# Attention scores from split q and k: a stacked two-pass product against three products on each head's own 64 rows

## The chip, the cores and the metric

The kernel runs on one core of one Trainium2 chip. The metric is device time in microseconds of one execution. TensorE (PE) multiplies matrices into PSUM, VectorE (DVE), ScalarE (ACT) and GpSimd (POOL) work on tiles, and SyncE (SP) issues nearly all DMA transfers, in order.

## What is computed

Softcapped attention over 4 batches, 12 heads, 448 positions and a head dimension of 64, then a bilinear feed-forward layer over all 1792 tokens:

```python
scores = scale * np.matmul(q, k.transpose(0, 1, 3, 2))
scores = cap * np.tanh(scores / cap)
attn = np.exp(scores - np.max(scores, axis=-1, keepdims=True))
attn = attn / (np.sum(attn, axis=-1, keepdims=True) + 1e-09)
x = np.matmul(attn, v)            # laid out as (1792, 768)
out = (x @ w_a) * (x @ w_b) @ w_out
```

q, k, v are f32. The weights arrive as 64-bit floats, and the kernel makes f32 out of them itself.

## The kernel before

**Precision.** A fp32r matmul passes once over its moving columns, at less than f32 precision. Where f32 precision is wanted, an operand x is split into a high part hi (x rounded to fp32r) and a low part lo = x - hi, and three one-pass products hi·hi, hi·lo and lo·hi are added up in PSUM. Matmuls on plain f32 tiles take several passes; the trace counts two instructions for each.

**Units of work.** The 48 heads are taken in 24 pairs, two heads A and B on partitions 0 to 63 and 64 to 127. Twelve pairs make a token group of 896 rows (`NG` = 2). The feed-forward of group 0 (`ffn(0)`) runs in slices between the steps of pairs 12 to 23, and that of group 1 (`ffn(1)`) runs behind the last pair. So there are three stages: attention alone (pairs 0 to 11), attention mixed with feed-forward and with the conversion of the weights, and feed-forward alone.

**Steps of one pair.** `load_pair` fetches q, k, v. `prep_pair` transposes q and k so that the head dimension lies on partitions, and splits them. `scores(pi, 0)` makes key chunks 0 and 1 (128 keys each) for both heads, `scores(pi, 1)` chunk 2 and the remainder of 64 keys. Each chunk goes into a PSUM tile `psc` of two banks, one per head (the remainder's two heads share one bank, one on each half of the partitions), and ACT takes tanh (L270) and then exp (L271). POOL and DVE add up the row sums in `psum`. `attend` (L293, L295) multiplies by v into `pv`, and `normalize` adds the sums over partitions (L308), takes the reciprocal (L316), spreads it through DRAM (`rd`, `den`), multiplies (L322) and splits the result into `xhi`, `xlo` (L331, L332) for the feed-forward.

**Transposes.** For pairs up to 12 (`pi < BLOCKED`) q and k are loaded with 112 partitions and transposed on PE against an identity (L232). From pair 13 on they are loaded in 32-wide column blocks (L206, eight issues), and one VectorE instruction per tensor transposes all 32x32 blocks (L223).

**Scores before.** `keys` holds for head A its high parts on rows 0 to 63 and its low parts on rows 64 to 127, for head B the other way round; `qhh` holds the high part of q on both halves. So one matmul over 128 rows (L263) gives hi·hi + lo·hi, and a second over the own 64 rows (L264) adds hi·lo. The other half of `qhh` is filled by a copy on DVE (L240, first two pairs) or by an SBUF-to-SBUF DMA (L242). The remainder's 64 keys of both heads take two matmuls over windows that reach into columns of zeros between the heads (L268), and a third with `kdiag`, the remainder's high parts on a diagonal (L269).

**Order.** The program's order for a pair is given by a string of steps, `"PASNFTF"` up to pair 12 and `"SFANPFTF"` after (P prep of the next pair, A and N attend and normalize of the pair before, S and T the two score halves, F a slice of feed-forward). The framework's scheduler puts each engine's instructions in order from there; on each engine they run in that order. `psc` tiles come from a pool of two (`ps_sc`), which from pair 12 on also holds `pv`; other PSUM tiles come from a pool of four (`ps_1`). Split q and k, `psum` and the probabilities are double-buffered.

**Weights.** In the first pass each of 36 weight tiles is converted (L389 to L394: two ACT, three DVE, one POOL instruction), written to DRAM, and split (L411, L412); in the second pass it is read back.

Of the kernel before, what the change touches and what calls it, by code (L numbers as in the profile page):

```python
# [9 lines left out]
F32 = mybir.dt.float32  # L10
# [106 lines left out]
def kernel(  # L117
# [66 lines left out]
    # [0 | B's first R] put both heads' remainders in one bank; kdiag has their high parts on its diagonal.  # L184
    koff, krem = (0, S + R), (MAIN, S + R)
    keys = [const.tile([P, 2 * S + R], F32R, tag=f"keys{i}", name=f"keys{i}") for i in range(2)]
    kdiag = [const.tile([P, P], F32R, tag=f"kdiag{i}", name=f"kdiag{i}") for i in range(2)]
    xhi = const.tile([P, NK, GT], F32R, tag="xhi", name="xhi")
    xlo = const.tile([P, NK, GT], F32R, tag="xlo", name="xlo")
    acc = const.tile([P, NTI, DM], F32, tag="acc", name="acc")  # L190

    un = lambda ap: ap.rearrange("d (p c) -> d c p", c=NCH)
    pm = lambda ap: ap.rearrange("d (c p) -> d c p", c=NCH)
    sides = ((slice(0, D), slice(D, P)), (slice(D, P), slice(0, D)))
    raw, stk, prob, pvs = {}, {}, {}, {}

    def load_pair(pi):
        b, hp = divmod(pi, NP)
        for nm, src in (("k", k), ("q", q)):
            if pi >= BLOCKED:  # L200
                t = ld.tile([P, S // BLK, BLK], F32, tag=f"ld{nm}", name=f"ld{nm}_{pi}")
                for j in range(2):
                    for h in range(D // BLK):
                        rows = slice(j * D + h * BLK, j * D + (h + 1) * BLK)
                        cols = src[b, 2 * hp + j, :, h * BLK : (h + 1) * BLK]
                        nc.sync.dma_start(t[rows], cols.rearrange("(c p) d -> p c d", p=BLK))  # L206
                raw[nm, pi] = t
                continue
            t = ld.tile([CP, NCH, 2, D], F32, tag=f"ld{nm}", name=f"ld{nm}_{pi}")
            for j in range(2):  # L210
                nc.sync.dma_start(t[:, :, j, :], src[b, 2 * hp + j].rearrange("(p c) d -> p c d", c=NCH))
            raw[nm, pi] = t
        t = ld.tile([P, 2 * NC3 + 1, D], F32, tag="ldv", name=f"ldv_{pi}", bufs=3)
        nc.sync.dma_start(t, v[b, 2 * hp : 2 * hp + 2].rearrange("j s d -> (j s) d").rearrange("(c p) d -> p c d", p=P))
        raw["v", pi] = t

    def prep_pair(pi):
        tk, tq = raw.pop(("k", pi)), raw.pop(("q", pi))
        blocked = pi >= BLOCKED
        if blocked:  # L220
            pk, pq = (qk.tile([P, S], F32, tag=f"t{nm}", name=f"t{nm}_{pi}", bufs=1) for nm in "kq")
            for p_, t in ((pk, tk), (pq, tq)):
                nc.vector.transpose(p_, t.rearrange("p c d -> p (c d)"))  # L223
        else:
            if pi >= NPG:
                both = ps_sc.tile([P, 2, 512], F32, tag="pssc", name=f"pt_{pi}")
                pk, pq = both[:, 0], both[:, 1]
            else:
                pk, pq = (ps_1.tile([P, 512], F32, tag="ps1", name=f"pt{nm}_{pi}") for nm in "kq")
            for p_, t in ((pk, tk), (pq, tq)):  # L230
                for c in range(NCH):
                    nc.tensor.transpose(p_[:, c * CP : (c + 1) * CP], t[:, c].rearrange("p j d -> p (j d)"), ident[:CP, :CP])  # L232
        khl, kdg = keys[pi % 2], kdiag[pi % 2]
        qhh = qk.tile([P, 2, S], F32R, tag="qhh", name=f"qhh_{pi}")
        qlo = qk.tile([P, S], F32R, tag="qlo", name=f"qlo_{pi}")
        to, fr = (lambda x: x, lambda x: x) if blocked else (un, pm)
        for j, (own, oth) in enumerate(sides):
            nc.scalar.copy(to(qhh[own, j]), fr(pq[own, :S]))
            if pi < 2:
                nc.vector.tensor_copy(un(qhh[oth, j]), pm(pq[own, :S]))  # L240
            else:
                nc.sync.dma_start(f32(qhh[oth, j]), f32(qhh[own, j]))  # L242
        for j, (own, oth) in enumerate(sides):
            kj = khl[:, koff[j] : koff[j] + S]
            nc.vector.tensor_copy(to(kj[own]), fr(pk[own, :S]))
            eng = nc.gpsimd if blocked else nc.vector
            eng.tensor_sub(to(kj[oth]), fr(pk[own, :S]), to(f32(kj[own])))
            nc.gpsimd.tensor_copy(kdg[own, j * R : (j + 1) * R], f32(khl[own, krem[j] : krem[j] + R]))
        for j, (own, oth) in enumerate(sides):
            nc.vector.tensor_sub(to(qlo[own]), fr(pq[own, :S]), to(f32(qhh[own, j])))  # L250
        stk[pi] = (khl, kdg, qhh, qlo)

    def scores(pi, hf):
        khl, kdg, qhh, qlo = stk[pi]
        pf = pp.tile([P, 4 - hf, S], F32, tag=f"pf{hf}", name=f"pf_{pi}_{hf}")
        for i in range(2):
            c = 2 * hf + i
            n = 2 if c < NC3 else 1
            psc = ps_sc.tile([P, 2, 512], F32, tag="pssc", name=f"psc_{pi}_{c}")
            if n == 2:  # L260
                for j, (own, _) in enumerate(sides):
                    kc = khl[:, koff[j] + j * R + c * P : koff[j] + j * R + (c + 1) * P]
                    nc.tensor.matmul(psc[:, j, :S], kc, qhh[:, j], start=True, stop=False)  # L263
                    nc.tensor.matmul(psc[:, j, :S], kc[own], qlo[own], start=False, stop=True)  # L264
            else:
                for j in range(2):
                    kc = khl[:, MAIN + j * R : MAIN + j * R + P]
                    nc.tensor.matmul(psc[:, 0, :S], kc, qhh[:, j], start=(j == 0), stop=False)  # L268
                nc.tensor.matmul(psc[:, 0, :S], kdg, qlo, start=False, stop=True)  # L269
            nc.scalar.activation(pf[:, 2 * i : 2 * i + n], psc[:, :n, :S], AF.Tanh, scale=capt[:, 1:2])  # L270
        nc.scalar.activation(pf, pf, AF.Exp, scale=capt[:, 0:1])  # L271
        prob[pi, hf] = pf
        t = psum[pi % 2]
        if hf == 0:
            nc.gpsimd.tensor_add(t, pf[:, 0:2], pf[:, 2:4])
        else:
            for j, (own, _) in enumerate(sides):
                nc.vector.scalar_tensor_tensor(  # L278
                    t[own, j], pf[own, 2], capt[own, 2:3], t[own, j], op0=ALU.add, op1=ALU.add
                )  # L280
            nc.gpsimd.tensor_add(t, t, pf[:, 0:2])  # L281

    def attend(pi):
        if pi >= NPG:
            both = ps_sc.tile([P, 2, 512], F32, tag="pssc", name=f"pv_{pi}")
            pvs[pi] = (both[:, 0], both[:, 1])
        else:
            pvs[pi] = (ps_1.tile([P, 512], F32, tag="ps1", name=f"pv_{pi}"), None)
        t, tv = pvs[pi][0], raw["v", pi]
        for c in range(NC3):  # L290
            for j in range(2):
                p = prob[pi, c // 2][:, 2 * (c % 2) + j]
                nc.tensor.matmul(t[j * D : (j + 1) * D, :S], tv[:, j * (NC3 + 1) + c], p, start=(c == 0), stop=False)  # L293
        for j, (own, _) in enumerate(sides):
            nc.tensor.matmul(t[own, :S], tv[own, NC3], prob[pi, 1][own, 2], start=False, stop=True)  # L295
        del prob[pi, 0], prob[pi, 1]

    def normalize(pi):
# [20 lines left out]
        for j, (own, _) in enumerate(sides):  # L319
            row = rd[pi][j * NCH : (j + 1) * NCH].rearrange("(o c) p -> o (c p)", o=1)  # L320
            nc.sync.dma_start(den[own], row.to_broadcast([D, S]))
        nc.vector.tensor_mul(den, t[:, :S], den)  # L322
        if g == 0:
            split_x(r, den, nc.gpsimd)
# [148 lines left out]
    with ExitStack():  # L473
# [100 lines left out]
```

## Time and profile before

| | us |
|---|---|
| median of 3 runs | 840.54 |
| lowest, highest | 838.63, 844.2 |
| profiled execution, first to last instruction | 838.4 |
| PE, DVE, ACT, POOL busy in it | 797.7, 545.9, 367.1, 342.6 |
| mean granted PE clock | 0.971 |

The profile gives for each engine the time in which it was busy. A PE that is busy is not PE at its peak: matmuls overlap, so the distance from one start to the next tells what one costs. A row of the timeline or of the groups names the source line, the engine, the operation, the tile written and the tiles read, the shape and the number of instructions; of a matmul, `64*128` means 64 rows of the array and 128 columns. What stands in brackets or behind the last bar is the idle time of the engine ahead of it and what ended it.

### The profile page before, as it was taken

Reading aid. Unit: us, or ns where it says so; the run is one execution under the profiler, and the core shown is the slowest. Engines: PE = TensorE matmul, PEld = TensorE weight load, DVE = VectorE, ACT = ScalarE, POOL = GpSimd, SP = SyncE. Lnnn points to the kernel's source line nnn. Section 1 sums busy time; section 2 is a strip of 40 time slices with the busy share of each in tenths; the row PEclk is TensorE's granted clock in tenths of the full one; section 3 lists DMA queues with packets and bytes.
Section 4 is the critical chain, followed back from the end, with each engine's and each line's share of the span. In section 5 each row is a group of like instructions: output and inputs, shape, how many; then the busy total and the mean of one; then the engine's idle time right before and its main releaser. Section 6 shows DMA issues by size and latency. Waiting matters only on the chain. (4 is left out here: it accounts for less than half of the span.)

```text
span 838.4 us, 10618 instructions
## 1 busy us (share of the span) xinstructions
PE 797.7 (95%) x3968; PEld 617.3 (74%) x3968; DVE 545.9 (65%) x670; ACT 367.1 (44%) x450; POOL 342.6 (41%) x224
## 2 busy tenths in 40 slices
PE   5999999899699889989989999999999999999997
PEld 3444443566478668758758767989999999999996
DVE  6788998979947986796696688285224343343514
ACT  4788886565654543553654463212331121212110
POOL 1366665777655653674564363211112020202000
PEclk9999999699799999999999999999999999999999
DMA  6244447766662653553543342454111111111003
GB/s 130 67 115 113 112 110 165 165 168 178 193 176 84 198 167 87 172 158 105 170 152 101 121 165 84 136 186 150 57 57 57 57 56 57 40 56 57 1 1 134
DMA packets 131320, 95.54 MB, mean 114 GB/s; under 512 B 91200, under 2 KB 118848, under 8 KB 131264
## 3 DMA queue, kind: packets, MB, share of 16 engines
q1 hardware_dynamic: 131264, 94.81, 39.5%
q8 instruction: 33, 0.54, 0.3%
q14 instruction: 23, 0.19, 0.1%
HBM read 67.24 MB, written 22.50 MB: 107 GB/s over the span
## 5 line engine op out<-in xcount | busy, mean ns | idle before, releaser
L460 PE MATMUL po<-who,gh 128*128 128x384 f32 x336 | 116.5, 350 | 8.3 <-DVE acc L466 6.1
L461 PE MATMUL po<-wlo,gh 128*128 128x384 f32 x336 | 115.1, 343 | 4.9 <-DVE wlo L412 4.9
L462 PE MATMUL po<-who,gl 128*128 128x384 f32 x336 | 111.6, 341 | 1.0 <-DVE gl L438 1.0
L429 PE MATMUL pha<-xhi,wha 128*128 128x448 f32 x288 | 107.6, 374 | 1.4 <-DVE xhi L331 1.4
L429 PE MATMUL phb<-xhi,whb 128*128 128x448 f32 x288 | 107.2, 372 | 0.0
L430 PE MATMUL pha<-xlo,wha 128*128 128x448 f32 x288 | 106.3, 369 | 0.0
L430 PE MATMUL phb<-xlo,whb 128*128 128x448 f32 x288 | 105.9, 368 | 0.0
L431 PE MATMUL pha<-xhi,wla 128*128 128x448 f32 x288 | 105.8, 369 | 0.0
L431 PE MATMUL phb<-xhi,wlb 128*128 128x448 f32 x288 | 105.8, 368 | 0.0
L270 ACT ACTIVATE pf<-psc,capt 128x896 f32<-128x896 f32 x96 | 85.0, 912 | 40.4 <-PE psc L264 38.6
L466 DVE TENSOR_TENSOR acc<-po,acc 128x384 f32<-128x384 f32 x140 | 74.5, 551 | 32.0 <-PE po L462 31.8
L412 POOL TENSOR_TENSOR wlb<-wrb,whb 128x768 fp32r<-128x768 f32 x12 | 22.2, 1848 | 154.9 <-PE pha L431 106.3
L271 ACT ACTIVATE pf<-pf,capt 128x1792 f32<-128x1792 f32 (+1 forms) x48 | 77.0, 1603 | 1.0
L460 PEld LDWEIGHTS po<-who,gh 128*128 128x128 f32 x336 | 64.5, 192 | 16.0 <-DVE acc L466 8.4
L436 DVE TENSOR_TENSOR asb<-phb,asb 128x448 f32<-128x448 f32 x48 | 29.7, 619 | 69.3 <-PE phb L431 69.3
L263 PE MATMUL psc<-qhh,keys 128*128 128x448 f32 x144 | 67.1, 467 | 4.5 <-DVE qhh L240 2.9
L434 ACT COPY asb<-pha 128x448 f32<-128x448 f32 x48 | 25.5, 530 | 104.0 <-PE pha L431 99.2
L293 PE MATMUL pv<-pf,ldv 128*64 128x448 f32 x288 | 68.2, 593 | 2.2 <-ACT pf L271 2.2
L281 POOL TENSOR_TENSOR psum<-psum,pf 128x896 f32<-128x896 f32 x24 | 52.3, 2180 | 43.7 <-DVE psum L278 28.5
L264 PE MATMUL psc<-qlo,keys 64*128 64x448 f32 x144 | 69.1, 482 | 0.5 <-DVE qlo L250 0.5
L461 PEld LDWEIGHTS po<-wlo,gh 128*128 128x128 f32 x336 | 64.6, 192 | 6.6 <-DVE wlo L412 6.0
L438 DVE TENSOR_TENSOR gl<-asb,gh 128x448 fp32r<-128x448 f32 x48 | 54.5, 1136 | 20.8 <-ACT gh L437 20.7
(103 smaller groups left out, 1459.6 us busy)
## 6 DMA issues: line engine op xcount, KB each, us to landing
w64a<-in_moe_w_a_dram SPq DMA_DIRECT2D x12, 768.0 KB
w64b<-in_moe_w_b_dram SPq DMA_DIRECT2D x12, 768.0 KB
w64o<-in_moe_w_out_dram SPq DMA_DIRECT2D x12, 768.0 KB
ldv<-in_v_dram SPq DMA_DIRECT2D x24, 224.0 KB
den<-rd SPq DMA_DIRECT2D x48, 112.0 KB
out_dram<-acc SPq DMA_DIRECT2D x13, 384.0 KB
qhh<-qhh SPq DMA_DIRECT2D x44, 112.0 KB
wda<-wta SPq DMA_DIRECT2D x12, 384.0 KB
```

Of the source, the lines that this page charges most:

```text
L263: nc.tensor.matmul(psc[:, j, :S], kc, qhh[:, j], start=True, stop=False)
L264: nc.tensor.matmul(psc[:, j, :S], kc[own], qlo[own], start=False, stop=True)
L270: nc.scalar.activation(pf[:, 2 * i : 2 * i + n], psc[:, :n, :S], AF.Tanh, scale=capt[:, 1:2])
L271: nc.scalar.activation(pf, pf, AF.Exp, scale=capt[:, 0:1])
L293: nc.tensor.matmul(t[j * D : (j + 1) * D, :S], tv[:, j * (NC3 + 1) + c], p, start=(c == 0), stop=False)
L429: nc.tensor.matmul(t[:, :S], wh[:, kk], xhi[:, kk, cs], start=(kk == 0), stop=False)
L430: nc.tensor.matmul(t[:, :S], wh[:, kk], xlo[:, kk, cs], start=False, stop=False)
L431: nc.tensor.matmul(t[:, :S], wl[:, kk], xhi[:, kk, cs], start=False, stop=(kk == NK - 1))
L460: nc.tensor.matmul(t[:, :HALF], gh[:, cs], wh, start=(f == fs[0]), stop=False)
L461: nc.tensor.matmul(t[:, :HALF], gh[:, cs], wl, start=False, stop=False)
L462: nc.tensor.matmul(t[:, :HALF], gl[:, cs], wh, start=False, stop=(f == fs[-1]))
L466: nc.vector.tensor_add(acc[:, ti, hs], t[:, :HALF], acc[:, ti, hs])
```

## The change

The score products are taken apart. `prep_pair` makes for each of q and k a transposed tile `tt`, a high part and a low part, all on 128 partitions with a head on each half. `scores` adds for each chunk and head three fp32r matmuls over the head's own 64 rows: hi·hi, hi·lo, lo·hi, and takes the two heads in turn within each product. The remainder takes one plain f32 matmul per head, with 64 rows and 64 columns, from the unsplit tiles. All pairs are loaded in 32-wide blocks and transposed on VectorE. `keys`, `kdiag`, `qhh`, the copies between halves (L240, L242, L248) and the PE transposes (L232) are gone. For k the high part is made on DVE and the low part on POOL, for q the high part on ACT and the low part on DVE.

```diff
     def load_pair(pi):
         b, hp = divmod(pi, NP)
         for nm, src in (("k", k), ("q", q)):
-            if pi >= BLOCKED:
...
-            t = ld.tile([CP, NCH, 2, D], F32, tag=f"ld{nm}", name=f"ld{nm}_{pi}")
+            t = ld.tile([P, S // BLK, BLK], F32, tag=f"ld{nm}", name=f"ld{nm}_{pi}")
             for j in range(2):
-                nc.sync.dma_start(t[:, :, j, :], src[b, 2 * hp + j].rearrange("(p c) d -> p c d", c=NCH))
+                for h in range(D // BLK):
+                    rows = slice(j * D + h * BLK, j * D + (h + 1) * BLK)
+                    cols = src[b, 2 * hp + j, :, h * BLK : (h + 1) * BLK]
+                    nc.sync.dma_start(t[rows], cols.rearrange("(c p) d -> p c d", p=BLK))
             raw[nm, pi] = t
...
     def prep_pair(pi):
-        tk, tq = raw.pop(("k", pi)), raw.pop(("q", pi))
...
+        stk[pi] = []
+        for nm in "kq":
+            t = raw.pop((nm, pi))
+            tt = qk.tile([P, S], F32, tag=f"t{nm}", name=f"t{nm}_{pi}")
+            nc.vector.transpose(tt, t.rearrange("p c d -> p (c d)"))
+            hi, lo = (qk.tile([P, S], F32R, tag=f"{nm}{x}", name=f"{nm}{x}_{pi}") for x in ("hi", "lo"))
+            if nm == "k":
+                nc.vector.tensor_copy(hi, tt)
+                nc.gpsimd.tensor_sub(lo, tt, f32(hi))
             else:
-                pk, pq = (ps_1.tile([P, 512], F32, tag="ps1", name=f"pt{nm}_{pi}") for nm in "kq")
...
+                nc.scalar.copy(hi, tt)
+                nc.vector.tensor_sub(lo, tt, f32(hi))
+            stk[pi].append((hi, lo, tt))
...
             if n == 2:
-                for j, (own, _) in enumerate(sides):
-                    kc = khl[:, koff[j] + j * R + c * P : koff[j] + j * R + (c + 1) * P]
-                    nc.tensor.matmul(psc[:, j, :S], kc, qhh[:, j], start=True, stop=False)
-                    nc.tensor.matmul(psc[:, j, :S], kc[own], qlo[own], start=False, stop=True)
+                for x, y in ((0, 0), (0, 1), (1, 0)):
+                    for j, o in enumerate(own):
+                        kk = tk[x][o, j * R + c * P : j * R + (c + 1) * P]
+                        nc.tensor.matmul(psc[:, j, :S], kk, tq[y][o], start=(x + y == 0), stop=(x == 1))
             else:
-                for j in range(2):
-                    kc = khl[:, MAIN + j * R : MAIN + j * R + P]
-                    nc.tensor.matmul(psc[:, 0, :S], kc, qhh[:, j], start=(j == 0), stop=False)
-                nc.tensor.matmul(psc[:, 0, :S], kdg, qlo, start=False, stop=True)
+                for j, o in enumerate(own):
+                    nc.tensor.matmul(psc[o, 0, :S], tk[2][o, krem[j] : krem[j] + R], tq[2][o], start=True, stop=True)
```

The other lines of the change rename the halves of the partitions and drop the zeroing of `keys` and `kdiag` at the start.

More of the change, by code (lines that the diff above doesn't have):

```diff
@@ L147 @@
     NC3 = S // P
-    MAIN = NC3 * P
-    R = S - MAIN
+    R = S - NC3 * P
     PFB = 2
@@ L155 @@
     BLK = 32
-    BLOCKED = NPG + 1
     dr = ctx.enter_context(tc.tile_pool(name="dr", bufs=1, space=bass.MemoryType.DRAM))
@@ L182 @@
     psum = [const.tile([P, 2, S], F32, tag=f"psum{i}", name=f"psum{i}") for i in range(2)]
-    koff, krem = (0, S + R), (MAIN, S + R)
-    keys = [const.tile([P, 2 * S + R], F32R, tag=f"keys{i}", name=f"keys{i}") for i in range(2)]
-    kdiag = [const.tile([P, P], F32R, tag=f"kdiag{i}", name=f"kdiag{i}") for i in range(2)]
     xhi = const.tile([P, NK, GT], F32R, tag="xhi", name="xhi")
@@ L190 @@
     acc = const.tile([P, NTI, DM], F32, tag="acc", name="acc")
-    un = lambda ap: ap.rearrange("d (p c) -> d c p", c=NCH)
-    pm = lambda ap: ap.rearrange("d (c p) -> d c p", c=NCH)
-    sides = ((slice(0, D), slice(D, P)), (slice(D, P), slice(0, D)))
+    own, krem = (slice(0, D), slice(D, P)), (S - R, 0)
     raw, stk, prob, pvs = {}, {}, {}, {}
@@ L217, in prep_pair @@
     def prep_pair(pi):
-        tk, tq = raw.pop(("k", pi)), raw.pop(("q", pi))
[L219 to L227, printed above, removed]
-            else:
-                pk, pq = (ps_1.tile([P, 512], F32, tag="ps1", name=f"pt{nm}_{pi}") for nm in "kq")
-            for p_, t in ((pk, tk), (pq, tq)):
-                for c in range(NCH):
-                    nc.tensor.transpose(p_[:, c * CP : (c + 1) * CP], t[:, c].rearrange("p j d -> p (j d)"), ident[:CP, :CP])
@@ L233, in prep_pair @@
[L233 to L250, printed above, removed]
@@ L253, in scores @@
     def scores(pi, hf):
-        khl, kdg, qhh, qlo = stk[pi]
+        tk, tq = stk[pi]
         pf = pp.tile([P, 4 - hf, S], F32, tag=f"pf{hf}", name=f"pf_{pi}_{hf}")
@@ L276, in scores @@
         else:
[L277 to L280, printed above, removed]
+            for j, o in enumerate(own):
+                nc.vector.scalar_tensor_tensor(t[o, j], pf[o, 2], capt[o, 2:3], t[o, j], op0=ALU.add, op1=ALU.add)
             nc.gpsimd.tensor_add(t, t, pf[:, 0:2])
@@ L293, in attend @@
                 nc.tensor.matmul(t[j * D : (j + 1) * D, :S], tv[:, j * (NC3 + 1) + c], p, start=(c == 0), stop=False)
-        for j, (own, _) in enumerate(sides):
-            nc.tensor.matmul(t[own, :S], tv[own, NC3], prob[pi, 1][own, 2], start=False, stop=True)
+        for o in own:
+            nc.tensor.matmul(t[o, :S], tv[o, NC3], prob[pi, 1][o, 2], start=False, stop=True)
         del prob[pi, 0], prob[pi, 1]
@@ L318, in normalize @@
         den = sm.tile([P, S], F32, tag="den", name=f"den_{pi}")
-        for j, (own, _) in enumerate(sides):
+        for j, o in enumerate(own):
             row = rd[pi][j * NCH : (j + 1) * NCH].rearrange("(o c) p -> o (c p)", o=1)
-            nc.sync.dma_start(den[own], row.to_broadcast([D, S]))
+            nc.sync.dma_start(den[o], row.to_broadcast([D, S]))
         nc.vector.tensor_mul(den, t[:, :S], den)
@@ L478 @@
         nc.vector.memset(sel, 0.0)
-        for i in range(2):
-            nc.gpsimd.tensor_scalar_mul(keys[i][:, S : S + R], ident[:, :R], 0.0)
-            nc.gpsimd.tensor_scalar_mul(kdiag[i], ident, 0.0)
         for m in range(2):
```

9 lines of the change are left out of this document (removed).

## The prediction

> **What bounds the kernel now.** I read the chain of work that ended last first, then busy time by stretch, then the timeline inside one stretch, and last the groups by shape.
>
> ```profile
> PE 37%; DVE 4%; issue 1%; DMA 1%; ACT 0%; POOL 0%; DVEq 0%
> 62.00:112.90 50.90, 50.90 (x279) 23.81 (x279) 45.88 (x56) 42.22 (x41) 31.16 (x26) 1.00 0.47 115
> 140.00:150.00 10.00, 7.79 (x22) 2.98 (x20) 9.94 (x8) 5.64 (x8) 8.97 (x6) 0.84 0.71 126
> 150.00:160.00 10.00, 10.00 (x38) 5.18 (x35) 9.83 (x12) 8.93 (x11) 5.53 (x5) 0.50 1.15 269
> 400.00:420.00 20.00, 20.00 (x108) 15.15 (x107) 14.23 (x15) 12.22 (x16) 10.01 (x6) 1.00 0.52 166
> ```
>
> The columns after the length are busy PE, weight load, DVE, ACT, POOL, then granted clock, DMA share, GB/s. There are three stages. From 62.00 to 112.90 us attention runs alone, five pairs of heads at 10.18 us each: PE is busy without a gap, but DVE is at 9.18 us per pair, ACT at 8.44 and POOL at 6.23, so PE can shrink only some 2 to 3 us before another engine binds. At 140 us, where weight conversion joins, DVE binds (9.94 of 10) and PE starves. From about 260 us to the end of attention near 530, PE is the limit again (20.00 of 20). One period of the first stage on PE:
>
> ```profile
> 75.98 0.60 PE L232 MATMUL ptk<-ident,ldk 112*128 112x112 f32 x4
> 76.73 0.45 PE L263 MATMUL psc<-qhh,keys 128*128 128x448 f32 x1
> 77.11 0.47 PE L264 MATMUL psc<-qlo,keys 64*128 64x448 f32 x1
> 77.51 0.47 PE L263 MATMUL psc<-qhh,keys 128*128 128x448 f32 x1
> ...
> 79.91 2.48 PE L293 MATMUL pv<-pf,ldv 128*64 128x448 f32 x12
> 82.31 0.97 PE L295 MATMUL pv<-pf,ldv 64*64 64x448 f32 x4
> 83.21 0.47 PE L263 MATMUL psc<-qhh,keys 128*128 128x448 f32 x1
> ...
> 84.81 0.68 PE L268 MATMUL psc<-qhh,keys 128*128 128x448 f32 x2
> 85.32 0.36 PE L269 MATMUL psc<-qlo,kdiag 128*128 128x448 f32 x1
> 85.61 0.59 PE L308 MATMUL sum<-psum,sel 128*32 128x112 f32 x16
> 86.14 0.60 PE L232 MATMUL ptk<-ident,ldk 112*128 112x112 f32 x4
> ```
>
> Starts are what counts, since matmuls overlap. Transposes: 75.98 to 76.73, 0.75 us. Eight score matmuls of chunks 0 and 1: to 79.91, 3.18 us. Attend: 2.40 and 0.90. Chunk 2 and the remainder: 83.21 to 85.61, 2.40 us. Row sums 0.53. Sum 10.16.
>
> **What a score matmul costs, and why.** L263 (128*128) and L264 (64*128) alternate at 0.40 us. In the FFN the same 448 columns pass in half of that:
>
> ```profile
> 414.22 0.37 PE L263 MATMUL psc<-qhh,keys 128*128 128x448 f32 x1
> 415.72 0.47 PE L429 MATMUL phb<-xhi,whb 128*128 128x448 f32 x1
> 416.03 0.36 PE L430 MATMUL phb<-xlo,whb 128*128 128x448 f32 x1
> 416.23 0.36 PE L431 MATMUL phb<-xhi,wlb 128*128 128x448 f32 x1
> ```
>
> Unchanged shape: 0.20 (416.03 to 416.23). First matmul after a change of shape: 0.31 (L429). Last before one: 0.29 (L269, 85.32 to 85.61). So a block of n slots of one shape costs about 0.2n + 0.2, and before, every slot of L263 and L264 is its own block.
>
> **PE after the change.** Chunks 0 to 2 become six products of 64 rows each, all 64*128, the heads in turn on rows 0 to 63 and 64 to 127 and in different banks. What they cost turns on whether two such tiles run side by side. No row shows 64*128 in pairs. The nearest are the column halves of L293 and the diagonal quarters of L295:
>
> ```profile
> 90.50 0.14 PEld L293 LDWEIGHTS pv<-pf,ldv 128*64 128x64 f32 x2 [0.23 <-issue]
> 92.47 0.20 PEld L295 LDWEIGHTS pv<-pf,ldv 64*64 64x64 f32 x4 [0.70 <-issue]
> L295 PEld LDWEIGHTS pv<-pf,ldv 64*64 64x64 f32 x96 | 4.9, 137 | 18.6 <-issue 18.6
> ```
>
> Four loads of 137 ns fit into 0.20 us, and two into 0.14: tiles on different rows or columns do overlap. Bounds for a pair of products: 0.20 (side by side), 0.40 (one after the other, one shape), 0.80 (with a change each). I take 0.20, as L295 is nearest: it has the very two row halves. Then chunks 0 and 1 cost 6 x 0.2 + 0.2 = 1.4, chunk 2 0.8. The remainder is two plain-f32 matmuls on the diagonal quarters, just what L295 does: 0.90. Scores are 3.1 instead of 5.58 us, the transposes go, and PE needs 10.16 - 5.58 - 0.75 + 3.1 = 6.9 us per pair.
>
> The two remainders go into one bank. L295 writes both its quarters into one bank too, and its loads and its 0.90 us are those of quarters side by side; were they to take turns, streaming would double, about 0.75 us more per pair (rival 4). The Trainium skill (TensorEngine Tiling (Array Packing), Gotcha 1: PSUM Pressure) speaks for the turns: different row tiles cannot access the same bank simultaneously. By it the time would be 797 instead of 788; the row of L295 does not bear it out for quarters on different columns.
>
> **The other engines in the first stage.**
>
> ```profile
> L247 DVE TENSOR_TENSOR keys<-ptk,keys 64x448 fp32r<-64x448 f32 x10 | 9.9, 988 | 0.3
> L250 DVE TENSOR_TENSOR qlo<-ptq,qhh 64x448 fp32r<-64x448 f32 x10 | 9.8, 981 | 0.2
> L245 DVE CAST keys<-ptk 64x448 fp32r<-64x448 f32 x10 | 9.3, 934 | 0.1
> L238 ACT CAST qhh<-ptq 64x448 fp32r<-64x448 f32 x10 | 9.4, 940 | 0.1
> L332 POOL TENSOR_TENSOR xlo<-den,xhi 128x448 fp32r<-128x448 f32 x5 | 5.7, 1145 | 6.5 <-DVE xhi L331 6.5
> L248 POOL CAST kdiag<-keys 64x64 fp32r<-64x64 f32 x10 | 4.6, 457 | 8.9 <-DVE keys L245 8.9
> L223 DVE STREAM_TRANSPOSE tk<-ldk 128x448 f32<-128x448 f32 x11 | 7.0, 632 | 0.1
> L437 ACT CAST gh<-asb 128x448 fp32r<-128x448 f32 x48 | 27.2, 566 | 77.3 <-DVE asb L436 77.1
> L331 DVE CAST xhi<-den 128x448 fp32r<-128x448 f32 x12 | 9.3, 779 | 0.4
> L245 DVE CAST keys<-tk 64x448 fp32r<-64x448 f32 x22 | 16.7, 759 | 3.9 <-PE psc L268 3.5
> L250 DVE TENSOR_TENSOR qlo<-tq,qhh 64x448 fp32r<-64x448 f32 x22 | 24.3, 1103 | 0.4
> ```
>
> ACT loses two casts of 0.94 and gains one of 0.566 (L437, the same shape): 8.44 - 1.88 + 0.57 = 7.1 us. DVE loses 2 x (0.988 + 0.981 + 0.934) = 5.8, gains two transposes of 0.632, one cast (L331, 0.78) and one subtraction (L250, 1.10; the time goes by columns, not rows): 9.18 - 5.8 + 3.1 = 6.5. POOL loses 2 x 0.457 and gains a subtraction like L332: 6.23 - 0.91 + 1.15 = 6.5. The limit becomes ACT at 7.1, with PE 6.9, DVE and POOL 6.5 just beneath it. Four engines so close, in order and with two score buffers, will not mesh fully; bounds for the period are 7.1 and 10.18 (nothing gained). I take 7.9, nearer the floor, since the present period lies at its own floor of PE. Over 11 periods that is 11 x (10.18 - 7.9) = 25 us.
>
> **DMA and SP.** The q and k loads of pairs 0 to 12 turn from four issues into eight, and the two copies of L242 per pair go: twelve issues per pair for ten.
>
> ```profile
> L206 SPq DMA_DIRECT2D ldk<-in_k_dram x44: 311/478/2137, 117.3 to 372.0; - x44
> L211 SPq DMA_DIRECT2D ldk<-in_k_dram x26: 562/603/811, 0.7 to 108.5; - x26
> 0.73 1.41 SPq L211 DMA_DIRECT2D ldk<-in_k_dram  x2
> 5.14 0.98 PE L232 MATMUL ptk<-ident,ldk 112*128 112x112 f32 x4 [5.14 <-DMA ldk<-in_k_dram]
> 16.80 1.91 ACT L270 ACTIVATE pf<-psc,capt 128x896 f32<-128x896 f32 x2 [2.95 <-PE psc L264]
> ```
>
> At the dearer 0.603 twelve are 7.2 us, under 7.9; at 0.478, 5.7. The row and den transfers behind the eight issues on SP may come up to four issues later, but den is wanted only by L322, two pairs of slack away. Loads are asked for two pairs ahead (16 us), which covers the smaller pieces at a DMA share of 0.47. With that cover gone a late q would cost its lateness once per pair.
> At the start nothing covers: k was issued by 2.14 and used at 5.14, 3.0 us later; eight issues at 0.6 end at 5.5, so q lands near 8.5. A transpose 0.63, a cast 0.57, a subtraction 1.1 and a chunk at the low clock of the start, about 2, bring the first tanh to some 12.8 instead of 16.80: 4 us gained (bounds 2 and 6).
>
> **The FFN stage.** Where PE binds, a chunk of four costs 1.50 (414.22 to 415.72) plus 0.11 on the next FFN matmul: three chunks 4.8, the remainder's three slots of one shape 0.6, together 5.4. After: 1.4 + 0.8 + 0.9 and about 0.2 at each of two entries, 3.5. Gain 1.9 per pair. Where DVE binds, a pair loses a cast (0.759) and a subtraction (1.103): 1.9 again; POOL and ACT get lighter too. Twelve pairs: 23 us (bounds 12 and 30).
>
> **Sum.** 838.4 - 25 - 4 - 23 = 786. The span of 838.4 stands 2.1 us under the median of the runs, 840.54, so the forecast is 788.
>
> **The rivals.**
> 1. *The row halves do not run side by side.* For it: no 64*128 pair in the trace. Against: L295. Then chunks 0 and 1 are 12 x 0.2 + 0.2 = 2.6, chunk 2 1.4, remainder 0.9: PE at 8.7 per pair in the first stage, 11 x 1.5 = 16 saved; in the FFN 0.1 per pair where PE binds (eight pairs) and 1.9 where DVE does (four): 8; the start 4. Time 812. The Trainium skill (TensorE: Matmul & The Clock Gate, Part 3) gives 3.07 times for four row tiles, which speaks against this one.
> 2. *Slower: each turn of the heads costs like a change of shape.* L263 and L264 at 0.40 speak for it; that L295 stays at one shape over both quarters speaks against. Eighteen products at 0.4 and 0.9 are 8.1 per pair, where 6.3 stood with transposes: 11 x 1.8 = 20 lost, in the FFN 12 x 2.9 = 35 lost, the start 4 gained: 892. The sign turns where a product costs about 0.29.
> 3. *PE falls to half clock.* At 140 to 150 PE was idle 2.2 us and the next stretch shows 0.50. PE no longer fills the first stage; with one window of 3.4 us at half speed per pair it needs 6.9 + 1.7 = 8.6, a period near 9: 12 us back, 800. Against: idle time is only 1 us per period, spread.
> 4. *The remainder's heads take turns.* 0.75 us more PE per pair: the first stage stays under its period (7.6), the FFN pairs lose 12 x 0.75 = 9: 797. Against it: L295's 0.90.
>
> **How the numbers follow.** My forecast 0.66, rival 1 0.12, rival 2 0.10, rival 3 0.08, rival 4 0.04. Low end 768: period at 7.1 (9 us), start and FFN at their better bounds (2 and 7). High end 818: rivals 4, 3 and 1 with a few us on top; rival 2 is left out. A measurement of this kernel (838.63 to 844.2) tells about 1% from no change. Faster by over 1%: 0.66 + 0.08 + 0.04 and 0.09 of rival 1's 0.12, 0.87; within 1% 0.03; slower 0.10.
>
> **What would show it.** Right: score matmuls 64*128 in pairs of nearly equal start, 0.2 us per pair; a period near 7.9 with ACT above 90%; the first tanh before 14; L223 from the first pair on. Wrong: starts 0.2 or 0.4 apart for the heads of a pair, a granted clock under 0.9 between 30 and 100 us, or DVE idle on ldq.

## The result and the profile after

| | before | after |
|---|---|---|
| median, us | 842.37 (838.63 to 844.45) | 809.8 (807.96 to 811.62) |
| ratio, 95% interval | | 0.9621 (0.9588 to 0.9655) |
| profiled execution, first to last instruction | 838.4 | 809.8 |

The kernel became 3.8% faster, by 32.6 us in the medians. The two profiled executions lie 28.6 us apart (after's is the slowest of its four, before's lies under its median). The forecast was 788, a gain of 52.

Busy time by stretch, after; columns as in the prediction, the stretches from 140 and 400 us the same:

```profile
30.00:90.00 60.00, 49.73 (x358) 19.78 (x356) 48.00 (x60) 46.96 (x47) 47.23 (x27) 0.94 0.54 105
140.00:150.00 10.00, 10.00 (x58) 5.51 (x57) 9.85 (x7) 3.14 (x5) 9.05 (x5) 1.00 0.62 167
400.00:420.00 20.00, 16.52 (x90) 13.58 (x87) 14.01 (x21) 5.58 (x6) 4.69 (x4) 0.83 0.35 114
```

In attention alone, where PE was busy without a gap, nobody is full now: PE 49.73, DVE 48.00, ACT 46.96 and POOL 47.23 of 60. At 140 us PE is now full, where it had 7.79 of 10. From 400 us, where PE was full, it now idles 3.5 us of 20 at a granted clock of 0.83. The stages, cut at four events of the trace (first exp, exp of the twelfth pair, first feed-forward matmul, first one of group 1); PE idle is the time between a matmul's end and the next start, half clock the time with a granted clock under 0.9:

| us | before | after | forecast change |
|---|---|---|---|
| start, to the first exp | 19.7 | 14.1 | -4 |
| attention alone, 11 periods | 115.6 | 95.5 | -25 |
| handover to the first feed-forward matmul | 22.1 | 18.4 | |
| feed-forward of group 0, with 12 pairs | 410.9 | 412.3 | -23 |
| of it PE idle, half clock | 21.8, 28.7 | 33.6, 34.1 | |
| feed-forward of group 1 | 270.1 | 269.6 | |

At the first feed-forward matmul 29.5 us were gained, almost as forecast (29), but partly by luck: attention alone gave 4.9 us less than forecast, the start 1.7 and the handover, for which no term stood, 3.7 more. From there on, where 23 more were due, nothing came. One period of the first stage on PE:

```profile
66.37 0.47 PE L230 MATMUL psc<-qhi,khi 64*128 64x448 f32 x2
66.67 0.37 PE L230 MATMUL psc<-qlo,khi 64*128 64x448 f32 x2
66.88 0.36 PE L230 MATMUL psc<-qhi,klo 64*128 64x448 f32 x2
67.17 0.97 PE L233 MATMUL psc<-tq,tk 64*64 64x448 f32 x4
68.07 0.59 PE L270 MATMUL sum<-psum,sel 128*32 128x112 f32 x16
68.59 1.72 PE L255 MATMUL pv<-pf,ldv 128*64 128x448 f32 x8
70.24 0.47 PE L230 MATMUL psc<-qhi,khi 64*128 64x448 f32 x2
...
71.65 0.60 PE L255 MATMUL pv<-pf,ldv 128*64 128x448 f32 x2
```

Each row holds both heads' products. They follow each other at 0.20 us (66.67 to 66.88): the two heads run side by side. The scores cost 1.41 (70.24 to 71.65), 0.80 (66.37 to 67.17) and 0.90 (67.17 to 68.07), 3.11 us where 3.1 were forecast. The remainder's two quarters share a PSUM bank and still take 0.90. So PE's part came out as worked out; what PE waits for did not. Waits between 30 and 90 us, in all, times, longest; the row of before, 30 to 112 us, for comparison:

```profile
PEld sum L270 <- POOL psum L243: 15.6, 7, 3.3
DVE den L284 <- DMA den<-rd: 11.9, 7, 2.4
PE sum L270 <- POOL psum L243: 10.2, 5, 2.5
```
```profile
PEld sum L308 <- POOL psum L275: 0.6, 2, 0.3
```

PE now stands before the row sums (L270) until POOL has added them up, and DVE stands before the multiply (L284) until the spread reciprocal has come through DRAM. Why POOL is late shows in the timeline, DVE and POOL of two periods:

```profile
26.07 0.35 DVE L212 CAST khi<-tk 128x448 fp32r<-128x448 f32 x1
...
33.55 2.11 POOL L239 TENSOR_TENSOR psum<-pf 128x896 f32<-128x896 f32 x1
34.11 1.80 DVE L212 CAST khi<-tk 128x448 fp32r<-128x448 f32 x1
35.83 2.15 DVE L242 SCALAR_TENSOR_TENSOR psum<-pf,capt,psum 64x448 f32<-64x448 f32 x2
36.06 1.45 POOL L213 TENSOR_TENSOR klo<-tk,khi 128x448 fp32r<-128x448 f32 x1 [0.40 <-DVE khi L212]
```

The same cast takes 0.35 us at 26.07, where POOL adds nothing, and 1.80 at 34.11, beside POOL's addition: that ends at 35.66, and the cast 0.25 us later. Then POOL, which needs the cast's result, has stood 0.40. The two engines take turns where the prediction had them side by side.

Before, this cost the first stage next to nothing, since there the splits read the transposed q and k from PSUM. DVE and POOL before the change:

```profile
91.48 2.11 POOL L281 TENSOR_TENSOR psum<-psum,pf 128x896 f32<-128x896 f32 x1 [0.77 <-DVE psum L278]
92.40 1.99 DVE L250 TENSOR_TENSOR qlo<-ptq,qhh 64x448 fp32r<-64x448 f32 x2
...
93.60 2.11 POOL L275 TENSOR_TENSOR psum<-pf 128x896 f32<-128x896 f32 x1
...
95.08 0.88 DVE L331 CAST xhi<-den 128x448 fp32r<-128x448 f32 x1
```

Two subtractions from PSUM (`ptq`) take 1.99 us beside POOL's addition, about 1 us each, and 0.95 to 0.98 us each with POOL idle. The cast from `den`, which lies in SBUF, stands: 0.88 us, ending 0.25 us after POOL. After the change all splits of q and k read SBUF, because VectorE transposes there. For the casts, subtractions and additions of DVE that read SBUF alone I added up what each took from 30 to 90 us beyond what it takes with POOL idle (cast 0.39, subtraction 0.62, addition to the sums 0.69 us): 14.7 us after the change, nothing before. This cost comes with the change itself, and the prediction has no term for it.

In the feed-forward stage the same happens in another place (400 to 407 us):

```profile
400.13 2.48 POOL L239 TENSOR_TENSOR psum<-pf 128x896 f32<-128x896 f32 x1
...
400.57 2.45 DVE L353 TENSOR_SCALAR wta<-w64a 128x768 int32<-128x768 int32 x1
...
404.93 1.95 DVE L428 TENSOR_TENSOR acc<-po,acc 128x384 f32<-128x384 f32 x4
...
405.54 0.69 PE L422 MATMUL po<-who,gh 128*128 128x384 f32 x1 [3.48 <-DVE acc L428]
...
406.02 0.52 PE L423 MATMUL po<-wlo,gh 128*128 128x384 f32 x1
...
406.34 0.52 PE L424 MATMUL po<-who,gl 128*128 128x384 f32 x1
```

A weight conversion (L353) stands beside POOL's addition, the accumulations (L428) come behind it and two more in DVE's queue, PE's PSUM buffers stay full for 3.48 us, and afterwards the output matmuls start 0.32 us apart (406.02 to 406.34), at a granted clock of 0.5 (from 404.03 to 410.85 us); at full clock they start 0.17 us apart.

### The profile page after: what moved, and what is told of

It reads as the page before. It is cut to its first block, busy times and chain, and to the rows that moved or that the text cites. A ratio compares the mean times of both kernels' runs of the same rounds, so it can differ in the third digit from the quotient of the medians.

```text
span 809.8 us, 10502 instructions
## 1 busy us (share of the span) xinstructions
PE 741.9 (92%) x4032; PEld 583.1 (72%) x4032; DVE 482.4 (60%) x618; ACT 340.9 (42%) x426; POOL 327.1 (40%) x174
## 5 line engine op out<-in xcount | busy, mean ns | idle before, releaser
L422 PE MATMUL po<-who,gh 128*128 128x384 f32 x336 | 121.3, 363 | 20.7 <-DVE acc L428 11.9
L424 PE MATMUL po<-who,gl 128*128 128x384 f32 x336 | 114.0, 348 | 1.9 <-DVE gl L400 1.9
L428 DVE TENSOR_TENSOR acc<-po,acc 128x384 f32<-128x384 f32 x140 | 74.9, 552 | 39.0 <-PE po L424 38.7
L422 PEld LDWEIGHTS po<-who,gh 128*128 128x128 f32 x336 | 66.5, 198 | 37.3 <-DVE acc L428 17.9
L243 POOL TENSOR_TENSOR psum<-psum,pf 128x896 f32<-128x896 f32 x24 | 58.5, 2437 | 33.5 <-DVE psum L242 30.8
L424 PEld LDWEIGHTS po<-who,gl 128*128 128x128 f32 x336 | 65.4, 196 | 2.9 <-DVE gl L400 2.8
L423 PEld LDWEIGHTS po<-wlo,gh 128*128 128x128 f32 x336 | 66.3, 197 | 0.9 <-DVE wlo L374 0.7
L391 PEld LDWEIGHTS pha<-xhi,wha 128*128 128x128 f32 x288 | 54.8, 190 | 12.2 <-DVE xhi L293 2.1
L393 PEld LDWEIGHTS pha<-xhi,wla 128*128 128x128 f32 x288 | 54.8, 190 | 8.9 <-POOL wla L374 2.6
```

The lines of the kernel that those rows point to most:

```text
L391: nc.tensor.matmul(t[:, :S], wh[:, kk], xhi[:, kk, cs], start=(kk == 0), stop=False)
L393: nc.tensor.matmul(t[:, :S], wl[:, kk], xhi[:, kk, cs], start=False, stop=(kk == NK - 1))
L422: nc.tensor.matmul(t[:, :HALF], gh[:, cs], wh, start=(f == fs[0]), stop=False)
L423: nc.tensor.matmul(t[:, :HALF], gh[:, cs], wl, start=False, stop=False)
L424: nc.tensor.matmul(t[:, :HALF], gl[:, cs], wh, start=False, stop=(f == fs[-1]))
L428: nc.vector.tensor_add(acc[:, ti, hs], t[:, :HALF], acc[:, ti, hs])
```

## The experiments

The theory after the result: (a) the products are as cheap as forecast, so PE isn't what holds the time; (b) the first stage is held by two loops of about the same length, one in which DVE and POOL take turns, and one from the row sums through the reciprocal, DRAM and the multiply back to DVE's queue; (c) in the feed-forward stage DVE's queue holds PE, so cheaper scores give nothing. The rival to (a) was that the order of the heads or the transposes alone make the gain, to (b) one loop alone or another limit, to (c) that the feed-forward term was simply too large.

**The heads one after the other.**

```diff
-                for x, y in ((0, 0), (0, 1), (1, 0)):
-                    for j, o in enumerate(own):
+                for j, o in enumerate(own):
+                    for x, y in ((0, 0), (0, 1), (1, 0)):
```

> The changed kernel with the order of the score products turned: all three of head A, then all three of head B, instead of the heads in turn. Theory (two 64-row products on different row halves run side by side, 0.20 us a pair): products of one head must follow each other, chunks 0 and 1 cost 12 x 0.2 + 0.2 = 2.6 instead of 1.4 us and chunk 2 1.4 instead of 0.8, so PE gains 1.8 us of work per pair; it shows in full only where PE sets the pace, so 820 to 840 us, with starts 0.2 us apart. Rival (the pairs only seem to start together, the time of a product is the same): within 4 us of the changed kernel's 810.

810.8 us, ratio 0.9658 (0.9619 to 0.9697), the same as after; the expectation of 820 to 840 failed. Its PE timeline:

```profile
61.14 0.48 PE L230 MATMUL psc<-qhi,khi 64*128 64x448 f32 x2
61.45 0.37 PE L230 MATMUL psc<-qlo,khi 64*128 64x448 f32 x2
61.65 0.38 PE L230 MATMUL psc<-qhi,klo 64*128 64x448 f32 x2
```

Head B's first product stands three behind head A's in the queue, yet each row still holds two products, 0.20 us apart from the next row. The two row halves run through their own work independently, so PE did not keep strictly to the order of its queue here; taking the heads in turn in the program isn't needed.

**The transposes alone**, in the kernel before.

```diff
-    BLOCKED = NPG + 1
+    BLOCKED = 0
...
-                nc.vector.tensor_copy(un(qhh[oth, j]), pm(pq[own, :S]))
+                nc.vector.tensor_copy(to(qhh[oth, j]), fr(pq[own, :S]))
```

> The kernel before with one part of the change: all pairs loaded in 32-wide blocks and transposed on VectorE; scores stay as they were. Theory (the score products carry the gain): PE loses 0.75 us of transposes per pair in the first stage, but POOL takes two key subtractions of 1.33 us per pair (6.2 + 2.7 = 8.9 us) and DVE keeps some 8.3, so a period between 9.4 and 10.2 instead of 10.18: 830 to 842 us. Rival (the transposes carry it): below 825.

844.64 us, ratio 1.0038 (0.9996 to 1.0081): nothing gained; the first stage takes 117.1 us. Moving the transposes alone doesn't make the gain. In this kernel it also gives POOL the two key subtractions per pair and lets DVE's splits read SBUF, so what the transposes on PE cost by themselves isn't shown.

**Lighter weight conversion**, in the kernel after and in the kernel before. Two of the three DVE instructions of each weight tile are left out: the one that puts sign and top exponent bit back, and the one that zeroes tiny values.

```diff
-        nc.vector.scalar_tensor_tensor(wt, hw, -0x40000000, wt, op0=ALU.bitwise_and, op1=ALU.bitwise_or)
-        nc.vector.scalar_tensor_tensor(f32(wt), ab, MIN_NORMAL_HI, f32(wt), op0=ALU.is_ge, op1=ALU.mult)
```

> The changed kernel without two of the three VectorE instructions of each weight's conversion (sign and zeroing are left out, so weights lose their sign): 72 instructions of 1.1 to 1.7 us less on DVE. To be compared with the next run, the kernel before with the same cut. Theory (the FFN stage gave nothing because DVE's queue, with the conversions ahead of the accumulations, set its pace): with the cut PE sets the pace, the gain of the change grows from 29 us to 40 to 50 us; this run 765 to 785. Rival (the gain of the FFN stage was lost on PE itself or in the order of work): the difference of the two stays between 25 and 33 us.

> The kernel before without two of the three VectorE instructions of each weight's conversion (sign and zeroing left out). Theory: PE already sets most of the pace, so it gains only what PE stood still and ran at half clock in the FFN stage: 810 to 825 us, and the changed kernel with the same cut is 40 to 50 us faster than this. Rival: the two lie 25 to 33 us apart.

783.65 us, ratio 0.9344 (0.9301 to 0.9388), and 818.97 us, ratio 0.977 (0.9716 to 0.9824). Busy time in the feed-forward of group 0, in this order: after and before, then after and before with light weights (columns: length, PE, PEld, DVE):

```profile
127.90:540.30 412.40, 378.80 (x1983) 292.51 (x1984) 289.00 (x345) 194.91 (x246) 199.42 (x98) 0.96 0.47 144
```
```profile
157.40:568.30 410.90, 389.09 (x1917) 300.98 (x1913) 311.84 (x359) 198.97 (x252) 222.38 (x128) 0.97 0.49 147
```
```profile
127.00:509.00 382.00, 367.62 (x1997) 282.35 (x1998) 206.13 (x276) 193.99 (x246) 184.89 (x97) 1.00 0.51 156
```
```profile
153.00:547.00 394.00, 384.01 (x1913) 298.46 (x1914) 226.11 (x290) 199.61 (x253) 208.34 (x127) 0.98 0.51 155
```

With 83 us less on DVE the changed kernel needs 383 us here instead of 412, though PE has the same matmuls (cut at the first feed-forward matmuls of the two groups, the light versions take 382.9 and 394.4 us): DVE does hold this stage, though it is busy only 70% of it. The change then gains 11.5 us in this stage instead of losing 1.4. That is in favour of (c) for about 13 us. The rest of the 23 did not come even there. In the medians the two gains differ by less: 35.3 us with light weights, 32.6 without, within their intervals. Neither the 40 to 50 of the theory nor the 25 to 33 of the rival came, and the split rests on one profile each.

**All 128 rows for each product**, so that two heads cannot run side by side. Each product then adds up over the rows of both heads, so the scores are not separated by head.

```diff
-                        kk = tk[x][o, j * R + c * P : j * R + (c + 1) * P]
-                        nc.tensor.matmul(psc[:, j, :S], kk, tq[y][o], start=(x + y == 0), stop=(x == 1))
+                        kk = tk[x][:, j * R + c * P : j * R + (c + 1) * P]
+                        nc.tensor.matmul(psc[:, j, :S], kk, tq[y], start=(x + y == 0), stop=(x == 1))
```

> The changed kernel with each score product taken over all 128 rows instead of the head's own 64, so that the two heads cannot run side by side (the scores then mix both heads; the remainder is unchanged). Chunks 0 and 1 cost 12 x 0.2 = 2.4 to 2.6 us instead of 1.4, chunk 2 1.2 to 1.4 instead of 0.8: PE 8.5 to 8.7 us per pair in the first stage, in the FFN stage 1.0 us more per pair. Theory (in the first stage PE is no longer the limit, and in the FFN stage only in part): most of it is hidden, 812 to 825 us. Rival (PE sets the pace throughout): 11 x 1.8 + 12 x 1.0 = 32 us more, 835 to 845.

808.58 us, ratio 0.9619 (0.9553 to 0.9685): no slower than after, where 812 to 825 was expected and 835 to 845 by the rival. Its PE timeline and busy time:

```profile
63.73 0.57 PE L230 MATMUL psc<-qlo,khi 128*128 128x448 f32 x2
64.14 0.57 PE L230 MATMUL psc<-qhi,klo 128*128 128x448 f32 x2
```
```profile
30.00:90.00 60.00, 59.27 (x365) 30.13 (x362) 46.14 (x60) 48.95 (x48) 46.27 (x27) 1.00 0.53 106
```

Two products now take 0.40 us instead of 0.20, PE is full again (59.27 of 60), and the first stage is 3.1 us longer (98.6). The feed-forward of group 0 is 7.4 us shorter (404.9): its scores take 13.3 us more of PE, but PE is idle for 25.6 instead of 33.6 us and at half clock for 20.5 instead of 34.1. PE's time is not scarce after the change; running side by side, correctly forecast, is worth nothing in the whole time. What is left for the gain is what both forms have: products of one shape, no PE transposes, no second copy of q, less work on DVE and ACT. It wasn't parted further.

**Loop one: the split of k without POOL.** High part on ACT, low part on DVE.

```diff
-                nc.vector.tensor_copy(hi, tt)
-                nc.gpsimd.tensor_sub(lo, tt, f32(hi))
+                nc.scalar.copy(hi, tt)
+                nc.vector.tensor_sub(lo, tt, f32(hi))
```

> The changed kernel with the split of k made as that of q: the high part cast on ACT, the low part subtracted on VectorE, nothing of it on POOL. Theory (in the first stage VectorE's cast L212 stands still, 1.76 instead of 0.4 us, while POOL adds sums, POOL then waits for it with L213, and the sums come late: POOL's chain of 8.5 us a pair is the period): POOL loses 1.45 us a pair and the cast's wait goes, the period falls from 8.7 to 7.4 to 8.0 us, so 797 to 804 us. Rival (order on PE): no change beyond 4 us, or slower as ACT gets 0.57 us more per pair.

807.52 us, ratio 0.9613 (0.9541 to 0.9684); the period is 8.4 us instead of 8.8, the first stage 92.3. Waits from 30 to 90 us:

```profile
DVE den L284 <- DMA den<-rd: 11.9, 7, 2.5
PE sum L270 <- POOL psum L243: 8.9, 6, 1.6
```

The time stays with the rival (no change beyond 4 us), not with the 797 to 804 of the theory. The wait for the reciprocal is all there, and POOL is still late. DVE did not get free of POOL either: the seven subtractions that replaced the casts took 9.9 us beyond their time with POOL idle, where the seven casts had taken 9.8.

**Loop two: later, further back, and without DRAM.** First `normalize` one pair later, with a third `psum`:

```diff
-                    normalize(pi - 1)
+                    if 1 < pi <= NPG:
+                        normalize(pi - 2)
+                    if pi >= NPG:
+                        normalize(pi - 1)
```

> The changed kernel with the row sums, reciprocal and normalization of a pair one pair later in the first stage (a third buffer for the sums), so that PE's row-sum matmuls L270 no longer stand in its queue waiting for POOL. Rival (PE's wait for the row sums, some 2 us in most periods with the pairs behind it in the queue, sets the period of the first stage): the 11 periods lose 8 to 12 us, 798 to 803 us. Theory (POOL and VectorE hold each other up in a loop of their own, and PE only shows it): the wait moves to another place, within 4 us of 810.

819.43 us, ratio 0.9744 (0.9679 to 0.9809), slower than after, which neither side had put down. PE no longer waits long for the sums, but DVE waits more, from 30 to 90 us:

```profile
DVE den L284 <- DMA den<-rd: 26.1, 6, 4.9
```

With the row sums late in the period, the reciprocal lands some 4.3 us after DVE has reached the multiply, and the transposes of the next pair stand behind it. Next the multiply alone (`spread`) one pair later, the transposes kept ahead of it:

```diff
+                    if 1 < pi <= NPG:
+                        spread(pi - 2)
...
+            if pi <= NPG:
+                tc.keep_in_program_order(tr)
```

> The changed kernel, complete, with VectorE's order in the first stage altered: the multiply by den comes behind the next pair's transposes and casts instead of ahead of them, some 2 us later behind its reciprocal. Theory (den's round trip in VectorE's queue sets the period): its wait of 1.8 us a pair is filled with that work, the period falls to 7.4 to 8.0 us, 798 to 804 us. Rival (POOL's sums, or ACT): within 4 us of 810.

818.75 us, ratio 0.9734 (0.9687 to 0.978), slower too, and again by neither side. The wait for the reciprocal is gone, and others came with the fixed order (30 to 90 us):

```profile
ACT qhi L217 <- DVE tq L209: 10.0, 6, 1.9
...
DVE psum L244 <- ACT pf L237: 8.5, 2, 5.2
```

Then the three transfers issued by ACT instead of SP:

```diff
-        nc.sync.dma_start(rd[pi], rec[0 : P : Q // 2])
+        nc.scalar.dma_start(rd[pi], rec[0 : P : Q // 2])
...
-            nc.sync.dma_start(den[o], row.to_broadcast([D, S]))
+            nc.scalar.dma_start(den[o], row.to_broadcast([D, S]))
```

> The changed kernel with the transfers rd and den issued from ACT's queue instead of SP's, where they stand between the eight issues of the next q and k. Theory (the issues on SP are part of the loop): if an issue costs ACT little, den comes about 1 us sooner, the period falls by 0.5 to 1 us, 799 to 806 us; if an issue costs ACT the 0.58 us that it costs SP, ACT's 7.1 us grow to 8.9 and it is slower, 812 to 820. Rival (the DMA's own 2 us each way are all of it): within 4 us of 810.

816.18 us, ratio 0.9685 (0.9642 to 0.9729). The wait fell from 11.9 to 9.8 us only, so SP's queue was a small part of it, and ACT paid for the issues: three took 0.59, 0.46 and 0.61 us in the period behind 61.8 us. The time is in the 812 to 820 put down for that case. Last, no spreading at all: the multiply takes a constant tile, so the output is not normalized.

```diff
-        nc.sync.dma_start(rd[pi], rec[0 : P : Q // 2])
...
-        nc.vector.tensor_mul(den, t[:, :S], den)
+        nc.vector.tensor_mul(den, t[:, :S], flat)
```

> The changed kernel without the way of the reciprocal row sums through DRAM: rd and den are not written or read, VectorE multiplies by a constant tile instead (so the output is not normalized), and three SP issues per pair go. Theory formed after the first runs (VectorE works in order, and its multiply L284 stands waiting for den, 1.8 us a pair, with the next pair's transposes behind it; reciprocal, two DMAs, multiply, transposes, reciprocal is a loop of 8.5 us that sets the first stage's period): the period falls from 8.7 to 7.2 to 7.8 us, where ACT's 7.1 us stop it, 10 to 16 us; in the FFN stage another 0 to 10: 785 to 800 us. Rival (POOL's sums set the period): over 804 us.

807.39 us, ratio 0.9602 (0.9555 to 0.965): the rival's time (over 804), not the theory's. POOL's timeline:

```profile
61.20 1.44 POOL L214 TENSOR_TENSOR klo<-tk,khi 128x448 fp32r<-128x448 f32 x1 [0.39 <-DVE khi L213]
63.29 2.42 POOL L244 TENSOR_TENSOR psum<-psum,pf 128x896 f32<-128x896 f32 x1 [0.65 <-DVE psum L243]
66.05 1.15 POOL L291 TENSOR_TENSOR xlo<-den,xhi 128x448 fp32r<-128x448 f32 x1 [0.33 <-DVE xhi L290]
67.15 2.12 POOL L240 TENSOR_TENSOR psum<-pf 128x896 f32<-128x896 f32 x1
69.66 1.44 POOL L214 TENSOR_TENSOR klo<-tk,khi 128x448 fp32r<-128x448 f32 x1 [0.39 <-DVE khi L213]
```

With loop two gone, the period settles at 8.5 us (61.20 to 69.66), and POOL's loop fills it: 1.44 + 2.42 + 1.15 + 2.12 of work and 0.65 + 0.33 + 0.39 in which it waits for a DVE instruction that had to wait for POOL. DVE, freed of the wait for the reciprocal, now stands beside POOL instead: from 30 to 90 us its instructions take 25.1 us beyond their time with POOL idle, after the change 14.7.

**Both loops at once**: the split of k without POOL, and the constant tile.

> Both suspected loops of the first stage are cut at once: the high part of k is made on ACT and its low part on DVE (no split of k on POOL), and the multiply takes a constant tile instead of the spread reciprocal, so the two transfers through DRAM and the wait for them are gone (the output is not normalized). Theory (two loops of about equal length, each alone keeps the period at 8.4 to 8.5): with both cut the period falls to 7.2 to 7.9, the first stage takes 80 to 87 us instead of 95.5, the first FFN half 398 to 402, and the time is 785 to 797. Rival (a third limit, such as ACT with one more cast of some 0.6 us, or DVE standing still while POOL adds sums, holds the period by itself): period 8.3 or more, first stage above 91 us, time 800 or more.

807.68 us, ratio 0.9623 (0.9574 to 0.9671). DVE's timeline, one period:

```profile
74.64 2.03 DVE L214 TENSOR_TENSOR klo<-tk,khi 128x448 fp32r<-128x448 f32 x1
76.59 1.37 DVE L243 SCALAR_TENSOR_TENSOR psum<-pf,capt,psum 64x448 f32<-64x448 f32 x2
...
79.19 1.64 DVE L290 CAST xhi<-den 128x448 fp32r<-128x448 f32 x1
80.74 0.63 DVE L210 STREAM_TRANSPOSE tk<-ldk 128x448 f32<-128x448 f32 x1
...
82.57 2.03 DVE L214 TENSOR_TENSOR klo<-tk,khi 128x448 fp32r<-128x448 f32 x1
...
93.53 0.56 DVE L350 TENSOR_SCALAR wta<-w64a 128x768 int32<-128x768 int32 x1 [1.00 <-DMA w64a<-in_moe_w_a_dram]
```

The period nearly came and the time did not. 74.64 to 82.57 is 7.93 us, just above the expected 7.2 to 7.9; DVE is now without a gap. Its own work would be 2.6 us shorter: the subtraction takes 2.03 instead of 0.63 us and the cast 1.64 instead of 0.39 as long as POOL adds. That each loop holds the period by itself, as the theory had it, isn't shown: in the mean over nine periods (table below) the cuts alone take off 0.38 and 0.56 us and both together 0.82, about their sum. Nor did a version end the turn-taking: with both cut, DVE's instructions still take 18.4 us of 60 beyond their time with POOL idle. The first stage took 98.4 us, not 80 to 87, and the whole time did not move, because other work came into the gap: the first weight conversion reaches DVE at 93.53 us instead of 116.30, pairs 10 and 11 then take 15.7 and 17.3 us each, and the first feed-forward matmul comes at 133.9 instead of 127.9.

| | mean of 9 periods | first conversion on DVE | first feed-forward matmul | feed-forward, group 0 | time |
|---|---|---|---|---|---|
| before | 10.26 | 139.4 | 157.5 | 410.9 | 842.37 |
| after | 8.76 | 116.3 | 127.9 | 412.3 | 809.8 |
| k off POOL | 8.38 | 112.5 | 125.0 | 409.5 | 807.52 |
| no round trip | 8.20 | 97.0 | 137.9 | 397.7 | 807.39 |
| both | 7.94 | 93.5 | 133.9 | 401.3 | 807.68 |

The three versions gain 3 to 7 us in nine periods and end within 2.5 us of after, less than their intervals allow to tell.

**A complete version with both**: the reciprocal spread by eight small matmuls on PE, against one column of the identity each, and copied out of PSUM.

```diff
+            for c in range(NCH):
+                nc.tensor.matmul(ts[o, c * CP : (c + 1) * CP], pick[o, c], rec[o], start=True, stop=True)
+        (nc.scalar.copy if g else nc.vector.tensor_copy)(den, ts[:, :S])
```

> A complete version: k is split on ACT and DVE as in the run before, and the reciprocal of the row sums is spread over the 64 rows by eight small PE matmuls against a chosen column of the identity instead of through DRAM, then copied out of PSUM (DVE in group 0, ACT in group 1). PE has about 0.9 us more per pair, DVE or ACT 0.5 us, SP three issues fewer. Theory: the wait for the spread reciprocal goes, the period is 7.8 to 8.2, the FFN half loses its waits too, and the time is 790 to 802, faster than the changed kernel (809.8). Rival (the added PE work and copy cost what the wait did, or another loop holds the period): 803 to 815.

819.09 us, ratio 0.9748 (0.9698 to 0.9797): slower than after, and beyond even the rival's 803 to 815. PE's timeline and busy time:

```profile
71.74 1.42 PE L283 MATMUL sum<-rec,pick 64*64 64x112 f32 x16
73.09 0.97 PE L256 MATMUL pv<-pf,ldv 128*64 128x448 f32 x4
```
```profile
30.00:100.00 70.00, 68.93 (x568) 33.64 (x566) 51.93 (x81) 60.75 (x65) 44.04 (x24) 1.00 0.51 101
```

The eight products (16 instructions, as f32 takes two) cost 1.35 us on PE (71.74 to 73.09), half as much again as the 0.9 put down, and PE is full once more at 68.93 of 70, at a period of 8.4. No version here beats the changed kernel by more than its interval.

## Why the prediction was right, and where it was wrong

The direction, the range and PE's part were right; the size was not, 32.6 us for 52. That the time lies in the range is in part luck. The step on which the forecast turned, products side by side, came true and yet did not make the gain: with products over all 128 rows the time is 808.6.

- *Products in pairs at 0.20 us, scores 3.1.* Right: 0.20 and 3.11. Rivals 1 and 2 (one after the other, a change of shape at each turn) and 4 (the remainder in turns) did not occur: 0.20 and 0.90 are their rows. The Trainium skill (TensorEngine Tiling (Array Packing), Gotcha 1: PSUM Pressure), which spoke for rival 4, differs from the measurement for two quarters on different columns, and the measurement decides: both heads' matmuls into the one bank started within 0.01 us of each other.
- *PE needs 6.9 per pair.* The starts above give 7.1: scores 3.11, row sums 0.52, attend 1.65 (68.59 to 70.24) and, for its later parts, 1.8.
- *The start, 4 us.* 5.7, inside its bounds.
- *A period of 7.9, 25 us.* Mean 8.76 over nine periods, and 20.1 us over the stage; ACT, to be above 90%, is at 78%. The step that failed is the list of floors: "DVE and POOL 6.5, just beneath", each engine for itself. Its price for the cast, 0.78, is the mean of twelve rows of L331, six of 0.39 with POOL idle and six of 0.81 to 2.28 beside POOL; the price of the subtraction, 1.10, mixes the two cases as well. So it took a mean over two cases where the new kernel, from 30 to 90 us, has the dearer one in all seven casts: beside an addition the cast stands, and POOL then stands for it.
- *"den is wanted only by L322, two pairs of slack away."* Wrong: DVE waited for it seven times in 60 us. What counts is not how far the use is in the program but what stands behind it in DVE's queue.
- *The feed-forward stage, 23 us.* This term failed, at +1.4, though the work was sized nearly right. DVE's busy time fell by 22.8 us (311.84 to 289.00). The score matmuls' distances from start to start, less idle time, add up to 36.7 us in this stage, before 56.7: 20.0 us saved, 1.8 per pair where 1.9 stood, over the 10.5 pairs or so whose matmuls the trace has in the stage (the scores of pair 12 come ahead of it). What failed is the step from there to the time. PE's idle time rose by 11.8 us, the output matmuls took 8.4 us more (107.5 for 99.1; 66 of 504 started at half clock, before 32) and the first of the two feed-forward products 2.2 us more. With 1.1 us of small gains elsewhere that is all of it. The prediction took the full stretch from 400 to 420 us for the whole, and had no term for PE waiting on DVE's queue.
- *Rival 3, half clock.* A part of it came: 6.8 us in the first stage instead of 3.4, with a clock of 0.94 between 30 and 90 us, not under 0.9, and more of it behind the gaps of the feed-forward stage.

What stays open: which parts of the change make the 20 us of the first stage; whether the turns of DVE and POOL alone set its period, as every version here keeps them; and whether the time from the first conversion to the end of group 0 has a floor of its own. Versions that reach it up to 23 us earlier end together, and less work on DVE shortens it, but the order of the conversions was not tried.

## What to carry to other kernels

When one engine gives up its place as the bound, the floors of the others are no longer enough: list who waits for whom among them, in order, and price each instruction by its rows beside the neighbour that it will have then. Look at where its operands lie, too: moving a transpose from PE to VectorE moved the splits from PSUM to SBUF, and beside POOL that changed their price. A stage's gain counts only if the next stage can take it; work that the scheduler puts into the gap may stand ahead of what the next stage needs. And a saving per unit is to be multiplied by the units in which its engine is the limit, not by all.

## What the runs showed of the hardware

- DVE's casts and subtractions between SBUF tiles of 128x448 stand while POOL runs an addition or a subtraction. In the changed kernel the cast of k takes 0.32 to 0.40 us with POOL idle and 0.93 to 1.81 beside it, always ending 0.25 us after POOL's instruction; the subtraction for q takes 0.63 with POOL idle and 1.05 to 2.55 beside it, ending 0.48 us after. Transposes (0.60 to 0.65 us) and the multiply that reads PSUM (0.58 to 0.63) take the same in both cases, and so did the casts from PSUM before (0.87 to 0.98). The Trainium skill (Advanced Engine Details and Errata, VectorE Performance Modes, Mode Summary) says that VectorE's second SBUF port is shared with GpSimd, so that GpSimd instructions and VectorE instructions that use both ports block each other. The casts agree with it and give the price; that sentence does not say whether it covers the subtractions, which stand as well.
- PE ran the two row halves independently of their order in the queue: in the run with the heads one after the other, head B's first product started 0.01 us after head A's, three places ahead of its turn. The Trainium skill (TensorEngine Tiling (Array Packing), Key Properties) has tiles that work in parallel; the trace agrees.
